# Linear attention and a Swish layer on one core: two groups of VectorE sums exchanged in the Y phase of block 6

## The chip, the cores and the metric

The kernel runs on one core of a Trainium2 chip. A core has five engines that run side by side, each with its own in-order queue: TensorE (PE, with its weight loads as PEld), VectorE (DVE), ScalarE (ACT), GpSimd (POOL) and SyncE (SP, which here only issues transfers). The metric is the device time in microseconds, the median of several runs of a kernel. The types that go in and out are float32; inside, the kernel works in bfloat16 with float32 sums.

## What is computed

Two layers, one behind the other. The first is a linear attention over 8 batches, 8 heads, 576 positions and a head size of 64; its result, laid out as 4608 tokens by 512, goes through a layer with 2048 hidden features.

```python
def phi(x): return np.where(x > 0, x, np.exp(x) - 1.0) + 1.0
q_p, k_p = phi(q), phi(k)
kv  = np.einsum('bhsd,bhse->bhde', k_p, v)
z   = np.sum(k_p, axis=2)
num = np.einsum('bhsd,bhde->bhse', q_p, kv)
den = np.einsum('bhsd,bhd->bhs', q_p, z)[..., None] + 1e-06
x   = (num / den) as 4608 x 512
h   = x @ w_in                          # 512 x 2048
g   = h * (1.0 / (1.0 + np.exp(-beta * h)))
out = g @ w_out                         # 2048 x 512
```

## The kernel before

**Blocks.** A batch has 576 = 9 x 64 positions. Eight ninths of a batch, 512 tokens, make one block, so blocks 0 to 7 are the batches 0 to 7; the last ninths of all eight batches together make block 8. The loop that starts at line 1074 runs b from 1 to 8 (B is 8). Each pass has two phases: H (`h_fast`, or `h_phase` for b = 1 and 2), which makes g from x, and Y (`y_fast`), which makes the output from g. The attention of a later batch is woven in: while block b runs, batch b + 1 gets its x (`numer_all`), and batch b + 2 its phi.

**How work is placed.** The order on each engine's queue is the order in which the program writes the instructions (`manual_schedule`); waits across engines follow from the data. Side work is put into two dictionaries, `sh` for the H phase and `sy` for the Y phase: `at(sy, n, f)` files f under slot n, and `run(side, n)` emits what lies there at a fixed point of the phase. So "slot 0 of Y" is a place in the program, and for VectorE's instructions a place in VectorE's queue.

**Products of sums.** Both matrix products save multiplications by a Strassen-like scheme: the operands are cut into halves, sums and differences of the halves are made on VectorE, and seven half-size products stand in for eight. In Y, all features take part. In H, from block 3 on, a part of the features does: the quarter 0 of w_in's columns in every block, and in the blocks 7 and 8 the quarter 2 as well (`h_products(b, 0)`, `h_products(b, 2)`). For these the kernel needs two sets of sums:

- `h_w_sums(fq)`, lines 797 to 803: four VectorE instructions that make the sums of w_in's quarter fq. They are made once: quarter 0 in block 2, quarter 2 ("w_in's second part") in the Y phase of block 6. The sums of quarter 2 are laid into the room of `vf`, the float32 buffer of v, which GpSimd's `v_copy` (L244) has read for the last time in block 5. They are first read in the second half of block 7's H phase, as `<-vf`.
- `h_x_sums(b)`, lines 811 to 822: four VectorE instructions (all at L822) that make the sums of block b's x, in the Y phase of the block before. They read `xT` (for block 8 `xT_tail`) and write the room of `xs_sb`. Block 7's H phase starts with a product of these sums: there `p0` (L837, tile `hz`) is the first thing on TensorE, while in the blocks 3 to 6 two full products (L405, tile `h_ps`) go ahead of it.

**Where x comes from.** `numer_all(b + 1)` runs at slot 10 of block b's H phase. VectorE divides (L351) and writes `xs_sb`; then SyncE issues four DMA transposes (L358) that carry `xs_sb` to `xT`. The x sums need their landing, both because they read `xT` and because they overwrite `xs_sb`. GpSimd's `tail_copy` (L371) takes the last ninth out of the same `xT`.

**The Y phase** (`y_fast`). TensorE runs seven products of 16 matmuls each (L1003), in the order ya, yd, ya, yc, yb, yd, yb. ScalarE copies ya into `r1` (L1018). VectorE then makes `u2` = yc + `r1` (L1026) and `u3` = yd + `u2` (L1027). The second use of yd writes the PSUM bank that u3 has read, so TensorE's sixth product waits for L1027. Then follow y2's two sums, L1036 ("the first sum of y") and L1039, and y1's L1047, with the stores between them. Slot 0 lies behind the copy into r1, so on VectorE ahead of u2; slot 4 lies between L1036 and the sixth product, so on VectorE ahead of L1039. Four PSUM banks (ya, yd, yc, yb) are handed on in turn to the first products of the next H phase.

Of the kernel before, what the change touches and what calls it, by code (L numbers as in the profile page):

```python
# [16 lines left out]
def kernel(  # L17
# [12 lines left out]
    B, H, S, D = q.shape  # L30
# [125 lines left out]
    def table(func):  # L156
        nc.scalar.activation(act0, warm[:, 0:1], func)  # L157
# [4 lines left out]
    def phi_exp(b, a, pr, x):  # L162
        e = work.tile([P, 2, J, D], BF16, tag="e", name="e", bufs=4)
        nc.scalar.activation(e, x, ACTF.Exp)  # L164
        st[b, a, pr, "e"] = e

    def phi_relu(b, a, pr, x):
        if pr == 0:
            st[b, a, "r"] = work.tile([P, 2, 2, J, D], BF16, tag="r", name="r")
        r = st[b, a, pr, "r"] = st[b, a, "r"][:, pr]  # L170
        nc.vector.tensor_scalar(r, x, 0.0, 1.0, ALU.max, ALU.add)  # L171

    def phi_tile(b, a):
        st[b, a] = work.tile([P, 2, J, P], BF16, tag=f"phi{a}", name=f"phi_{a}", bufs=1)

    def phi_min(b, a, pr):
        nc.vector.tensor_tensor(  # L177
            st[b, a][:, pr].rearrange("p j (h d) -> p j h d", h=2),
            st[b, a, pr, "e"].rearrange("p h j d -> p j h d"),
            st[b, a, pr, "r"].rearrange("p h j d -> p j h d"),  # L180
            ALU.min,
        )

    def xin(b, a, pr):
        if b == 0:
            return x0f[pr if a == "q" else 2 + pr]
        return (xk if a == "k" else xq)[b % 2][:, 2 * pr : 2 * pr + 2]

    def phi_part(b, a, pr):
        x = xin(b, a, pr)  # L190
        phi_exp(b, a, pr, x)
        phi_relu(b, a, pr, x)
        phi_min(b, a, pr)
# [11 lines left out]
    def v_copy(eng, b, pr):  # L205

        copy(
            eng, vaug[b % 2][:, pr, :, :, 0:D],
            (v0b if b == 1 else vf)[:, 2 * pr : 2 * pr + 2].rearrange("p h j d -> p j h d"),
        )  # L210
# [5 lines left out]
    def kv_both(b):  # L216

        t = banks("kvp")
        for pr in range(2):
            for j in range(J):
                for il in range(2):
                    for a in range(2):
                        nc.tensor.matmul(  # L226
                            t[half(il), a, pr * EA : (pr + 1) * EA],
                            st[b, "k"][half(a), pr, j, il * D : (il + 1) * D],
                            vaug[b % 2][half(a), pr, j, il, 0:EA],
                            start=(j == 0), stop=(j == J - 1), skip_group_check=True,  # L230
                        )
        tv = t[:, :, 0 : 2 * EA].rearrange("p a (r e) -> p a r e", r=2)
        if b > 1:
            nc.vector.tensor_copy(kv_q[b % 2], tv)
            return
        st[b, "kv"] = kv_bd.rearrange("p a r h e -> p a r (h e)")
        for il in range(2):
            copy((nc.scalar, nc.vector)[il], kv_bd[half(il), :, :, il], tv[half(il)])
# [34 lines left out]
    def q_trans_dma(b):  # L273
        st[b, "qTd"] = work.tile([P, 2, 2 * J, G], BF16, tag="qT", name="qTd", bufs=1)
        for hh in range(2):
            nc.sync.dma_start_transpose(
                out=st[b, "qTd"][:, hh],
                in_=st[b, "q"][half(hh)].rearrange("p a j c -> p (a j c)"),
            )
# [90 lines left out]
    def tail_copy(b):  # L370
        nc.gpsimd.tensor_copy(  # L371
            xT_tail[:, :, b].rearrange("p i r n -> p i (r n)"), xT[b % 2][:, :, 8]
        )
# [99 lines left out]
    def w_sum(k):  # L473

        for n in range(2):
            r = slice(4 * n, 4 * n + 4)
            a, b = (
                (wq(n, HM), wq(n, 0)),
                (wq(2 + n, HM), ws[0][:, r]),
                (wq(2 + n, HM), wq(n, HM)),  # L480
                (wq(2 + n, 0), ws[1][:, r]),
            )[k]
            nc.vector.tensor_sub(ws[k][:, r], a, b)
# [253 lines left out]
    def at(side, n, *fs):  # L737
        side.setdefault(n, []).extend(fs)
# [54 lines left out]
    def h_w_plain(fq, f, r):  # L793

        return w_in_sb[fq][:, 2 * r : 2 * r + 2, f * 256 : (f + 1) * 256]

    def h_w_sums(fq):

        s, a = h_w[fq], lambda f, r: h_w_plain(fq, f, r)
        nc.vector.tensor_add(s[:, 0], a(1, 0), a(1, 1))  # L800
        nc.vector.tensor_sub(s[:, 1], s[:, 0], a(0, 0))
        nc.vector.tensor_sub(s[:, 2], a(0, 0), a(1, 0))
        nc.vector.tensor_sub(s[:, 3], a(0, 1), s[:, 1])

    def h_x_plain(b, r, t):

        if b == B:
            return xT_tail[:, :, 4 * t : 4 * t + 4, r]
        return xT[b % 2][:, :, 4 * t + r : 4 * t + 4 : 2]

    def h_x_sums(b):

        t = [h_xs[:, k] for k in range(4)]
        x = lambda r, t: h_x_plain(b, r, t)

        def like(a, c):
            return a.rearrange("p i (t n) -> p i t n", n=c.shape[-1])

        for k, (u, w) in enumerate((
            (x(0, 1), x(0, 0)), (x(1, 1), t[0]), (x(1, 1), x(0, 1)), (x(1, 0), t[1])  # L820
        )):
            nc.vector.tensor_sub(like(t[k], u), u, like(w, u) if k % 2 else w)  # L822
# [236 lines left out]
    def next_loads(b):  # L1059

        for pr in range(2) if b == 2 else ():
            v_copy(nc.gpsimd, b, pr)
        if b + 1 < B:
            if b == 3:
                load_v(b + 1)
            nc.gpsimd.tensor_copy(gate, st[b, "qTd"][:, 1, 2 * J - 1, G - 1 : G])
            if b != 3:
                load_v(b + 1)
            if b > 2:
                load_qk(b + 1)  # L1070
            for pr in range(2) if b > 2 else ():
                v_copy(nc.gpsimd, b + 1, pr)

    for b in range(1, B + 1):
        n, m = b + 1, b + 2
        sh, sy = {}, {}
        if b == 2 or b == B - 1:
            at(sh, 0, lambda: tail_copy(b))
        if n < B:
            at(sh, 0, lambda: next_loads(n))  # L1080
            if b > 2:
                at(sh, 0, lambda: tail_copy(b))
            at(sh, {1: 9, 2: 3}.get(b, 0), lambda: kv_both(n))
            at(sh, {1: 11, 2: 5}.get(b, 10), lambda: numer_all(n))
        if b == 1:
            at(sh, 4, lambda: w_sum(2))
            at(sh, 9, lambda: w_sum(1))
            at(sy, 0, lambda: w_sum(3))
        if m < B:
            at(sy, 0, lambda: phi_tile(m, "q"), lambda: phi_tile(m, "k"))  # L1090
            if b == 1:

                for pr in range(2):
                    at(sy, 0, lambda pr=pr: phi_exp(m, "q", pr, xin(m, "q", pr)))
                    at(sy, 2, lambda pr=pr: phi_relu(m, "q", pr, xin(m, "q", pr)))
                    at(sy, 3 + pr, lambda pr=pr: phi_min(m, "q", pr))
                for pr in range(2):
                    at(sy, 0, lambda pr=pr: v_copy(nc.scalar, m, pr))
                at(sy, 4, lambda: q_trans_dma(m))
                for pr in range(2):  # L1100
                    at(sy, 5, lambda pr=pr: phi_exp(m, "k", pr, xin(m, "k", pr)))
                    at(sy, 5, lambda pr=pr: phi_relu(m, "k", pr, xin(m, "k", pr)))
                    at(sy, 6, lambda pr=pr: phi_min(m, "k", pr))
                at(sy, 6, lambda: table(ACTF.Silu))
            else:
                at(sy, 0, lambda: phi_part(m, "q", 0))
                at(sy, 1, lambda: phi_part(m, "q", 1))
                at(sy, 1, lambda: q_trans_dma(m))
                at(sy, 4, lambda: phi_part(m, "k", 0))
                at(sy, 4, lambda: phi_part(m, "k", 1), lambda: table(ACTF.Silu))  # L1110
        if b == 2:
            at(sh, 2, lambda: h_w_sums(0))
        if b == B - 2:
            at(sy, 4, lambda: h_w_sums(2))
        if 2 <= b < B:
            at(sy, 6 if b < B - 2 else 0, lambda: h_x_sums(n))
        (h_phase if b < 3 else h_fast)(b, xT[b % 2] if b < B else xT_tail, sh)
        y_fast(b, sy)

# [29 lines left out]
```

## Time and profile before

| | us |
|---|---|
| three runs, median | 273.45 |
| lowest, highest | 273.04, 274.24 |
| the profiled execution, its time | 273.47 |
| its span in the profile | 271.7 |

In the profile each time is in microseconds from the start of the span. A row of a timeline reads: start, busy time, engine, line, instruction, result <- operands, shapes, count, and in brackets the idle time of that engine ahead of it with what ended it. A row such as `DVE xs_sb L822` in the chain of waits names the engine, the tile written and the line. The queues of issuing engines carry a q (SPq). The granted clock of TensorE was 0.999 of full speed over the span. Matmuls are pipelined and the profile models their ends, so distances between starts are safer than busy times.

### The profile page before, as it was taken

Reading aid. Unit: us, or ns where it says so; the run is one execution under the profiler, and the core shown is the slowest. Engines: PE = TensorE matmul, PEld = TensorE weight load, DVE = VectorE, ACT = ScalarE, POOL = GpSimd, SP = SyncE. Lnnn points to the kernel's source line nnn. Section 1 sums busy time; section 2 is a strip of 40 time slices with the busy share of each in tenths; the row PEclk is TensorE's granted clock in tenths of the full one; section 3 lists DMA queues with packets and bytes.
Section 4 is the critical chain, followed back from the end, with each engine's and each line's share of the span. In section 5 each row is a group of like instructions: output and inputs, shape, how many; then the busy total and the mean of one; then the engine's idle time right before and its main releaser. Section 6 shows DMA issues by size and latency. Waiting matters only on the chain.

```text
span 271.7 us, 6793 instructions
## 1 busy us (share of the span) xinstructions
PE 263.0 (97%) x2859; PEld 181.3 (67%) x2865; DVE 207.1 (76%) x404; ACT 167.4 (62%) x236; POOL 43.6 (16%) x65
## 2 busy tenths in 40 slices
PE   7799999999999999999999999999999799999994
PEld 3485455446865587658765876588658666886793
DVE  4871786999996579689968986899686877856862
ACT  5738894977965893599349934994492038405810
POOL 5922005040105003030213003310000100000000
PEclk9999999999999999999999999999999999999999
DMA  7999999997599945995699559945504050023013
GB/s 252 240 207 351 249 320 249 273 183 258 90 247 191 187 78 99 281 210 72 109 257 232 85 91 273 232 86 96 148 7 85 0 154 4 0 51 106 0 41 116
DMA packets 49214, 42.19 MB, mean 155 GB/s; under 512 B 30352, under 2 KB 41248, under 8 KB 49184
## 3 DMA queue, kind: packets, MB, share of 16 engines
q0 software_dynamic: 13296, 22.81, 37.3%
q1 hardware_dynamic: 35568, 18.75, 31.0%
q8 instruction: 22, 0.36, 0.5%
q10 hardware_dynamic: 320, 0.20, 0.2%
q14 instruction: 8, 0.07, 0.1%
HBM read 36.71 MB, written 9.44 MB: 170 GB/s over the span
## 4 chain that ended last, share of the span: by engine, by line
PE 89%; DMA 4%; DVE 2%; SPq 2%; issue 1%; ACT 0%; DVEq 0%; ACTq 0%
PE h_ps L405 36%; PE yd L1003 10%; PE ya L1003 9%; PE yb L1003 8%; PE hc L837 5%; PE yc L1003 5%; PE y_ps L420 4%; PE hz L837 4%; DMA stage<-in_k_dram 3%; PE kvp L226 2%; PE nps L336 2%; DMA xT<-xs_sb 2%; PE yb L975 1%; SPq L358 1%; PE xtp L385 1%
## 5 line engine op out<-in xcount | busy, mean ns | idle before, releaser
L413 ACT ACTIVATE g<-h_ps,beta_c 128x512 bf16<-128x512 f32 x112 | 74.6, 690 | 63.0 <-PE h_ps L405 62.5
L405 PE MATMUL h_ps<-xT,w_in 128*128 128x512 bf16 (+1 forms) x464 | 97.6, 357 | 0.1
L405 PEld LDWEIGHTS <-w_in 128*128 128x128 bf16 x496 | 44.8, 98 | 40.7 <-issue 0.2
L1003 PEld LDWEIGHTS <-stage 128*128 128x128 bf16 x480 | 47.0, 98 | 5.5
L1003 PEld LDWEIGHTS <-g 128*128 128x128 bf16 x384 | 37.5, 98 | 7.6 <-issue 1.6
L1003 PE MATMUL ya<-w_out,g 128*128 128x256 bf16 x256 | 30.6, 273 | 0.0
L351 DVE TENSOR_TENSOR xs_sb<-nps,rden 128x448 bf16<-128x448 f32 (+2 forms) x24 | 18.2, 758 | 0.8
L164 ACT ACTIVATE e<-xk 128x1152 bf16<-128x1152 bf16 (+1 forms) x15 | 16.7, 1159 | 0.2 <-DMA xk<-in_k_dram 0.2
L1003 PE MATMUL yd<-ws,g 128*128 128x256 bf16 x128 | 15.3, 273 | 1.4 <-DVE u L1027 1.4
L164 ACT ACTIVATE e<-xq 128x1152 bf16<-128x1152 bf16 x14 | 15.6, 1160 | 0.0
L157 ACT ACT_TABLE_LOAD x12 | 15.4, 1283 | 0.2
L1003 PE MATMUL yc<-ws,stage 128*128 128x256 bf16 x128 | 15.3, 273 | 0.0
L1003 PE MATMUL yd<-ws,stage 128*128 128x256 bf16 x128 | 15.3, 273 | 0.0
L244 POOL CAST vaug<-vf 128x1152 bf16<-128x1152 f32 x10 | 11.4, 1175 | 22.1 <-DMA vf<-in_v_dram 22.1
L420 PE MATMUL y_ps<-w_out,g 128*128 128x512 bf16 x60 | 14.4, 379 | 0.3 <-issue 0.2
L887 ACT ACTIVATE g<-hc,beta_c 128x512 bf16<-128x512 f32 x16 | 10.1, 683 | 6.4 <-DVE hc L873 6.4
L177 DVE TENSOR_TENSOR phi_q<-e,r 128x1152 bf16<-128x1152 bf16 x16 | 12.1, 757 | 2.3 <-ACT e L164 1.3
L177 DVE TENSOR_TENSOR phi_k<-e,r 128x1152 bf16<-128x1152 bf16 x16 | 12.7, 802 | 1.5 <-DVE r L171 0.5
L746 DVE TENSOR_TENSOR stage<-g 128x1024 bf16<-128x1024 bf16 x16 | 11.0, 686 | 3.2 <-ACT g L413 3.2
L1003 PE MATMUL yb<-w_out,stage 128*128 128x256 bf16 x112 | 13.4, 272 | 0.0
L1003 PE MATMUL yb<-ws,stage 128*128 128x256 bf16 x112 | 13.4, 273 | 0.0
L837 PEld LDWEIGHTS <-w_in 128*128 128x128 bf16 x96 | 9.4, 98 | 4.5
(139 smaller groups left out, 359.2 us busy)
## 6 DMA issues: line engine op xcount, KB each, us to landing
out_dram<-y SPq DMA_DIRECT2D x29, 256.0 KB, 3.8
vf<-in_v_dram POOLq DMA_DIRECT2D x6, 1152.0 KB, 9.1
xq<-in_q_dram POOLq DMA_DIRECT2D x7, 576.0 KB, 12.4
xk<-in_k_dram POOLq DMA_DIRECT2D x7, 576.0 KB, 14.5
w_in<-in_moe_w_in_dram POOLq DMA_DIRECT2D x4, 512.0 KB, 11.7
g<-in_moe_w_out_dram POOLq DMA_DIRECT2D x2, 1024.0 KB, 17.2
stage<-in_moe_w_out_dram POOLq DMA_DIRECT2D x2, 1024.0 KB, 20.9
stage<-in_q_dram SPq DMA_DIRECT2D x2, 576.0 KB, 4.2
```

Of the source, the lines that this page charges most:

```text
L157: nc.scalar.activation(act0, warm[:, 0:1], func)
L164: nc.scalar.activation(e, x, ACTF.Exp)
L177: nc.vector.tensor_tensor(st[b, a][:, pr].rearrange("p j (h d) -> p j h d", h=2), st[b, a, pr, "e"].rearrange("p h j d -> p j h d"), st[b, ...
L244: eng.tensor_copy(dst, src)
L351: nc.vector.tensor_mul(xs_sb[:, ils, v0 * D : v1 * D].rearrange("p i (u d) -> p i u d", d=D), pv[:, :, :, 0:D], rden[:, :, :, None].to_bro ...
L405: nc.tensor.matmul(hp[:, c0:c1].rearrange("p (t n) -> p t n", n=n), w_in_sb[ff // 4][:, kc, (ff % 4) * P : (ff % 4 + 1) * P], xm, start=(k ...
L413: nc.scalar.activation(g_sb[b % 2][:, ff, :], hp, ACTF.Silu, scale=beta_c[:, ff : ff + 1])
L420: nc.tensor.matmul(yp[:, c0:c1], g_sb[b % 2][:, ff, t * P : (t + 1) * P], w_out_sb[i][:, c, c0:c1], start=(ff == 0), stop=(ff == FC - 1), ...
L746: nc.vector.tensor_add(gs[0][:, c], g[:, c, HM:512], g[:, c2, HM:512])
L837: nc.tensor.matmul(o, lhs[:, i, a * P : (a + 1) * P], m, start=(first and a == 0 and i == 0), stop=True, skip_group_check=True,)
L887: nc.scalar.activation(g_sb[b % 2][:, ff].rearrange("p (t n) -> p t n", t=2), src, ACTF.Silu, scale=beta_c[:, ff : ff + 1],)
L1003: nc.tensor.matmul(ps[:, p * HM : (p + 1) * HM], lhs(c, p), rhs(c), start=(first and p == 0 and c == 0), stop=True, skip_group_check=True,)
```

## The change

In the Y phase of block 6 the two groups of VectorE sums change places. The sums of w_in's quarter 2 go from slot 4 to slot 0, and the sums of block 7's x from slot 0 to slot 4. In the Y phase of block 7 the sums of block 8's x stay in slot 0, and in the blocks 2 to 5 the x sums stay in slot 6.

```diff
         if b == B - 2:
-            at(sy, 4, lambda: h_w_sums(2))
+            at(sy, 0, lambda: h_w_sums(2))
         if 2 <= b < B:
-            at(sy, 6 if b < B - 2 else 0, lambda: h_x_sums(n))
+            at(sy, {B - 2: 4, B - 1: 0}.get(b, 6), lambda: h_x_sums(n))
```

## The prediction

> **What bounds the kernel now.** I read the page's engine shares and its chain of work first, then the chain piece by piece around the Y phase of block 6, then the timelines of VectorE, SyncE and TensorE there, and last block 7, which already has the order that block 6 is to get. From the page, engine shares and the chain:
>
> ```profile
> span 271.7 us, 6793 instructions
> PE 263.0 (97%) x2859; PEld 181.3 (67%) x2865; DVE 207.1 (76%) x404; ACT 167.4 (62%) x236; POOL 43.6 (16%) x65
> ...
> PE 89%; DMA 4%; DVE 2%; SPq 2%; issue 1%; ACT 0%; DVEq 0%; ACTq 0%
> ```
>
> TensorE bounds the kernel; only some 11% of the chain lies elsewhere. The columns of the chain in order of time are start, length (both us), and what:
>
> ```profile
> 206.28 4.34 DMA xT<-xs_sb
> ...
> 210.74 0.44 DVE xs_sb L822
> ...
> 212.37 0.61 DVE u L1026
> ...
> 213.01 0.70 DVE u L1027
> ...
> 213.75 1.91 PE yd L1003 x16
> 215.66 1.75 PE yb L1003 x16
> 217.41 0.44 PE hz L837 x4
> ```
>
> Here the chain leaves TensorE: the transposes of batch 7's x land at about 210.62, VectorE's four x sums (L822) follow, then u2 (L1026) and u3 (L1027), and only then TensorE's yd product starts. The timelines of the three engines, with the waits in brackets (VectorE, SyncE, TensorE; start, busy us):
>
> ```profile
> 207.38 0.69 DVE L748 TENSOR_TENSOR stage<-g,stage 128x1024 bf16<-128x1024 bf16 x1
> ...
> 210.74 0.43 DVE L822 TENSOR_TENSOR xs_sb<-xT 128x512 bf16<-128x512 bf16 x1 [2.67 <-DMA xT<-xs_sb]
> 211.20 0.50 DVE L822 TENSOR_TENSOR xs_sb<-xT,xs_sb 128x512 bf16<-128x512 bf16 x1
> ...
> 212.29 0.68 DVE L1026 TENSOR_TENSOR u<-yc,r 128x512 f32<-128x512 f32 x1
> 213.01 0.69 DVE L1027 TENSOR_TENSOR u<-yd,u 128x512 f32<-128x512 f32 x1
> 213.79 0.69 DVE L1036 TENSOR_TENSOR y<-yb,u 128x512 f32<-128x512 f32 x1
> 214.40 0.41 DVE L800 TENSOR_TENSOR vf<-w_in 128x512 bf16<-128x512 bf16 x1
> ...
> 215.52 0.42 DVE L803 TENSOR_TENSOR vf<-w_in,vf 128x512 bf16<-128x512 bf16 x1
> 215.86 0.69 DVE L1039 TENSOR_TENSOR y<-yd,u 128x512 f32<-128x512 f32 x1
> ```
>
> ```profile
> 202.39 5.15 SPq L358 DMA_TRANSPOSE xT<-xs_sb  x4
> ```
>
> ```profile
> 208.69 1.91 PE L1003 MATMUL yc<-ws,stage 128*128 128x256 bf16 x16
> 210.44 1.91 PE L1003 MATMUL yb<-ws,stage 128*128 128x256 bf16 x16
> 213.75 1.91 PE L1003 MATMUL yd<-ws,g 128*128 128x256 bf16 x16 [1.40 <-DVE u L1027]
> 215.50 1.91 PE L1003 MATMUL yb<-w_out,stage 128*128 128x256 bf16 x16
> 217.24 0.60 PE L837 MATMUL hz<-xs_sb,h_w 128*128 128x256 bf16 x4
> ```
>
> VectorE ends its g sums at 207.38 + 0.69 = 208.07 and stands 2.67 us with x sums at its head that wait for the landing. TensorE pays for 1.40 us of that. The profile models the ends of matmuls, so I count by starts: yc to yb is 210.44 - 208.69 = 1.75 us for 16 matmuls, but yb to yd is 213.75 - 210.44 = 3.31 us. The stall is worth 3.31 - 1.75 = **1.56 us**. Block 7, same timelines, where the x sums at this place are of data long landed:
>
> ```profile
> 234.69 0.69 DVE L748 TENSOR_TENSOR stage<-g,stage 128x1024 bf16<-128x1024 bf16 x1
> 235.30 0.42 DVE L822 TENSOR_TENSOR xs_sb<-xT_tail 128x512 bf16<-128x512 bf16 x1
> ...
> 236.43 0.42 DVE L822 TENSOR_TENSOR xs_sb<-xT_tail,xs_sb 128x512 bf16<-128x512 bf16 x1
> 237.25 1.91 PE L1003 MATMUL yb<-ws,stage 128*128 128x256 bf16 x16
> 237.52 0.69 DVE L1026 TENSOR_TENSOR u<-yc,r 128x512 f32<-128x512 f32 x1 [0.67 <-PE yc L1003]
> 238.25 0.69 DVE L1027 TENSOR_TENSOR u<-yd,u 128x512 f32<-128x512 f32 x1
> 239.00 1.91 PE L1003 MATMUL yd<-ws,g 128*128 128x256 bf16 x16
> 239.20 0.69 DVE L1036 TENSOR_TENSOR y<-yb,u 128x512 f32<-128x512 f32 x1 [0.26 <-PE yb L1003]
> ```
>
> There u2 starts 0.27 us behind the start of yb, u3 0.73 behind u2, and yd starts 239.00 - 237.25 = 1.75 us behind yb: no stall.
>
> **The change part by part.** Nothing is added: VectorE's four x sums and four w sums of block 6 change places; no matmul, DMA or wait of another engine's own is new.
>
> *The w sums, to the place ahead of u2.* They need only w_in, loaded at the start, and the room in vf, last read by POOL's copies of batch 7's v, long ago:
>
> ```profile
> 172.51 2.24 POOL L244 CAST vaug<-vf 128x1152 bf16<-128x1152 f32 x2 [7.10 <-DMA vf<-in_v_dram]
> ...
> 210.74 0.69 POOL L371 COPY xT_tail<-xT 128x256 bf16<-128x256 bf16 x1 [27.39 <-DMA xT<-xs_sb]
> ```
>
> So they should start at 208.07 + 0.04. They last from 214.40 to 215.52 + 0.42 = 215.94 today, 1.54 us, and would end at 209.65. Queued behind them is u2, which can't start before 210.44 + 0.27 = 210.71, when yc is done. They lie wholly in a 2.6 us gap, with 1.06 us to spare: cost nothing. Without that cover each 0.1 us past 1.06 would be 0.1 us on yd.
>
> *u2 and u3.* u2 at 210.71, u3 at 211.44, ended 212.13; in block 6 today yd follows the end of u3 (213.01 + 0.69 = 213.70) by 0.05, so u3 allows yd at 212.18, and TensorE's own pace allows it at 210.44 + 1.75 = 212.19. This is the tightest place of the forecast, 0.01 us, but block 7's rows carry the same distances without a stall. yd moves from 213.75 to 212.19: gain 1.56.
>
> *The x sums, behind y2's first sum.* L1036 starts 0.20 us behind yd in block 7, so 212.39; but u3 has VectorE until 212.13, so it isn't held up, and the next instruction starts 214.40 - 213.79 = 0.61 later, at 213.00. The landing (210.62) is 2.4 us past by then, so the wait has gone, not moved. The sums take 236.43 + 0.42 - 235.30 = 1.55 us in block 7 and end at 214.55. Who waits? First, block 7's opening product hz (L837), which reads the second sum: it is due 217.24 - 213.75 = 3.49 us behind yd, at 215.68, 1.1 us after the last sum. Second, y's sum L1039, queued behind them on VectorE: yd's result is ready at 212.19 + 1.75 + 0.20 = 214.14, so it starts about 0.4 us late, at 214.55, and ends at 215.24. That sets back an output store, on which nothing waits, and a PSUM bank that block 7's first full h_ps reuses; this one starts behind the four hz matmuls (0.44 us by the chain), at 216.12, 0.88 us later. Today the w sums stand at this same spot with nearly the same length, so this is no new burden. Cost nothing; gone cover would cost what exceeds 0.88 us.
>
> *A neighbour that is new.* POOL's tail copy starts when the transposes land, at 210.74, beside the x sums today and beside u2 (210.71) afterwards. Today's x sums beside it took 0.43 and 0.50 us, 0.42 in block 7. Block 1 shows u2 beside such a copy (timeline):
>
> ```profile
> 73.21 0.69 DVE L1026 TENSOR_TENSOR u<-yc,r 128x512 f32<-128x512 f32 x1 [0.26 <-PE yc L1003]
> 73.26 0.40 POOL L371 COPY xT_tail<-xT 128x256 bf16<-128x256 bf16 x1 [11.46 <-DMA xT<-xs_sb]
> ```
>
> u2 keeps its 0.69 us. The price lies between nothing and the copy's whole 0.69 us; I take nothing, by block 1's row, the same pair of instructions. The Trainium skill's page "SBUF — State Buffer" (section "Who interferes with whom") speaks of this pair of engines: a VectorE instruction with two inputs in SBUF and a GpSimd one that reads SBUF exclude each other for a whole instruction, while one with at most one SBUF input outside the 2-port modes doesn't contend. u2 reads one operand from PSUM, so by that rule too the sum stays at 1.56; the same rule would have today's x sum or the copy wait out the other, whereas the rows show both starting at 210.74, with at most some tenths of a microsecond added to either.
>
> *Behind it.* From 213.75 on, by stages (busy time of PE, PEld, DVE, ACT, POOL, the granted clock, DMA share and rate):
>
> ```profile
> 213.75:268.00 54.25, 54.19 (x448) 42.46 (x447) 38.79 (x65) 22.42 (x36) 0.00 (x0) 1.00 0.16 46
> ```
>
> TensorE is busy 54.19 of 54.25 us at full clock, so what starts 1.56 us earlier ends 1.56 us earlier; the transfers left in that stretch are stores.
>
> **The sum.** Profiled execution: 273.47 us (span 271.7, 1.77 around it). 273.47 - 1.56 + 0 + 0 + 0 = 271.91. The median of the runs shown is 273.45, 0.02 below the profiled one, so I predict **271.9 us**.
>
> **The rivals.**
>
> *Part of the gain is lost at u2 (chance 0.07).* POOL's copy holds u2 for up to 0.69 us; u3 has no slack, so yd comes that much later: gain 0.87, 272.6 us. For it: the 0.01 us of margin, and the lengthened copy (0.69 against 0.40). Against it: the rows of block 1.
>
> *The stall was hidden anyway (0.05).* If something later had been waiting with a time of its own, the 1.56 us would turn into a new gap in block 7, and the time would stay at 273.4. For it: the tail ends in stores, and VectorE is 76% busy. Against it: the stage row above, where TensorE never rests, and L1039 as the last thing that the swap sets back, with 0.88 us of room.
>
> *The w sums block VectorE's queue (0.06): slower.* VectorE is in order. Its first w sum carries a wait today that costs nothing, because all is over by 213.8 (the instructions of that line):
>
> ```profile
> L800 DVEq EVENT_SEMAPHORE  x1: 21/21/21, 213.8 to 213.8; - x1
> ```
>
> At 208.07 it could be unmet. The one late event of the neighbourhood is POOL's tail copy, which ends at 210.74 + 0.69 = 211.43. If the wait covered it, the sums would run 211.47 to 213.01, u2 and u3 (213.70 - 212.29 = 1.41 us) to 214.42 and yd start at 214.47, 0.72 later than now: 274.2 us. It decides from 209.16 on (u2's 210.71 less 1.55 us): a wait that lasts beyond costs one for one, and makes the kernel slower than now once it passes 210.74. Against it: the vf room was last read at 172.51 + 2.24 = 174.75, and the tail copy of batch 7 stands later in the program than these sums.
>
> *The change doesn't do what it says:* only if slot 0 were emitted elsewhere; it is run behind ya's copy and ahead of pd, as L822 shows by its present place. No chance of its own.
>
> **How the numbers follow.** The forecast has 0.82, the rivals 0.07, 0.05 and 0.06. A measurement of this kernel can tell about 0.5%, or 1.37 us, from no change, and 1.56 lies just above it. The three runs before span 1.2 us (273.04 to 274.24), and the landing that ended the stall took 4.34 us in this one execution; where it takes less, the old kernel stalls less. I give the forecast 0.78 to be seen above the bound: 0.82 x 0.78 = 0.64 faster. The rest of it, 0.18, with 0.07 and 0.05, is 0.30 within the bound, and 0.06 slower. The range: the three runs less 1.56 give 271.5 to 272.7, the first rival 272.6; I widen the ends by 0.2 for the unknown state of the landing: 271.3 to 272.9. Outside lie most of the 0.05 and 0.06 and about a tenth of the forecast.
>
> **What would show it.** In the changed profile: four sums vf<-w_in starting near 208.1 with no wait worth naming, u2 near 210.7 ended by yc, no gap ahead of yd (1.75 us behind yb), x sums near 213.0 without a wait for the DMA, hz 5.24 us behind yb's start, and a span near 270.1. A wait of VectorE ahead of the w sums, a u2 over 0.7 us or started late, or a gap ahead of hz or h_ps of block 7 would show the rivals, and a chain that leaves TensorE again later than yd would prove the forecast wrong.

## The result, and the profile after

| | before | after |
|---|---|---|
| runs, median (lowest to highest), us | 273.31 (273.04 to 274.24), 6 runs | 271.78 (271.67 to 271.92), 6 runs |
| ratio after / before, 95% interval | | 0.9944 (0.9934 to 0.9954) |
| profiled execution, time and span, us | 273.47 and 271.7 | 271.76 and 270.0 |

The kernel became 1.53 us faster by the medians, 0.56%; the forecast was 271.9 us. Below, one run is left out of its median: with both groups in slot 4, one of six runs took 276.74 us, at a granted clock of 0.994. The page of the changed kernel:

```profile
span 270.0 us, 6793 instructions
PE 263.6 (98%) x2859; PEld 181.8 (67%) x2865; DVE 206.5 (77%) x404; ACT 167.4 (62%) x236; POOL 43.0 (16%) x65
```

The instruction counts are those of before. The busy times differ by 0.6 us at most; TensorE's share of the shorter span has grown from 97% to 98%, VectorE's from 76% to 77%. The chain of waits of the changed kernel around block 6's Y phase (start, length, what):

```profile
208.70 1.75 PE yc L1003 x16
210.45 1.75 PE yb L1003 x16
212.20 1.75 PE yd L1003 x16
213.94 1.75 PE yb L1003 x16
215.69 0.44 PE hz L837 x4
```

Where SyncE, the landing and VectorE stood in the chain before, it now runs through TensorE without a break. Its timeline, VectorE, POOL and TensorE together (start, busy us, waits in brackets):

```profile
207.22 0.69 DVE L748 TENSOR_TENSOR stage<-g,stage 128x1024 bf16<-128x1024 bf16 x1
207.83 0.42 DVE L800 TENSOR_TENSOR vf<-w_in 128x512 bf16<-128x512 bf16 x1
...
208.96 0.42 DVE L803 TENSOR_TENSOR vf<-w_in,vf 128x512 bf16<-128x512 bf16 x1
210.29 1.91 PE L1003 MATMUL yb<-ws,stage 128*128 128x256 bf16 x16
210.56 0.69 DVE L1026 TENSOR_TENSOR u<-yc,r 128x512 f32<-128x512 f32 x1 [1.18 <-PE yc L1003]
210.59 0.40 POOL L371 COPY xT_tail<-xT 128x256 bf16<-128x256 bf16 x1 [27.44 <-DMA xT<-xs_sb]
211.28 0.69 DVE L1027 TENSOR_TENSOR u<-yd,u 128x512 f32<-128x512 f32 x1
...
212.03 1.91 PE L1003 MATMUL yd<-ws,g 128*128 128x256 bf16 x16
212.24 0.69 DVE L1036 TENSOR_TENSOR y<-yb,u 128x512 f32<-128x512 f32 x1 [0.26 <-PE yb L1003]
212.84 0.41 DVE L822 TENSOR_TENSOR xs_sb<-xT 128x512 bf16<-128x512 bf16 x1
...
213.97 0.42 DVE L822 TENSOR_TENSOR xs_sb<-xT,xs_sb 128x512 bf16<-128x512 bf16 x1
214.30 0.68 DVE L1039 TENSOR_TENSOR y<-yd,u 128x512 f32<-128x512 f32 x1
...
215.53 0.60 PE L837 MATMUL hz<-xs_sb,h_w 128*128 128x256 bf16 x4
```

The w sums start straight behind the last g sum. u2 now waits for TensorE (1.18 us), not TensorE for u2: yd stands 212.03 - 210.29 = 1.74 us behind yb, where it was 3.31. The landing still comes at about the same place, as POOL's copy at 210.59 shows, but VectorE reaches the x sums 2.3 us after it.

The span fell by 1.7 us, somewhat more than the stall. The rest is not of the change: the Y phase of block 6 itself began earlier (ya at 203.30 against 203.45). The two rows, before and after:

```profile
203.45 1.91 PE L1003 MATMUL ya<-w_out,g 128*128 128x256 bf16 x16
```

```profile
203.30 1.91 PE L1003 MATMUL ya<-w_out,g 128*128 128x256 bf16 x16
```

The stretch from that ya to the end of the span leaves this out: 271.7 - 203.45 = 68.25 us before, 270.0 - 203.30 = 66.70 after, so **1.55 us** for the change. Below, "Y6 to the end" is this stretch. Spans are given to 0.1 us, so a stretch is good to about 0.05 us and a difference of two to about 0.1.

### The profile page after: what moved, and what is told of

Read it like the earlier page. It is cut to its first block, busy times and chain, and to the rows that moved or that the text cites. A ratio compares the mean times of both kernels' runs of the same rounds, so it can differ in the third digit from the quotient of the medians.

```text
span 270.0 us, 6793 instructions
## 1 busy us (share of the span) xinstructions
PE 263.6 (98%) x2859; PEld 181.8 (67%) x2865; DVE 206.5 (77%) x404; ACT 167.4 (62%) x236; POOL 43.0 (16%) x65
## 4 chain that ended last, share of the span: by engine, by line
PE 94%; DVE 2%; DMA 1%; ACT 1%; issue 1%; DVEq 0%
PE h_ps L405 36%; PE ya L1003 10%; PE yd L1003 10%; PE yb L1003 9%; PE hc L837 5%; PE yc L1003 5%; PE y_ps L420 5%; PE hz L837 4%; PE kvp L226 2%; PE nps L336 2%; DMA stage<-in_q_dram 1%; PE yb L975 1%; PE xtp L385 1%; DVE r L171 1%; DVE phi_q L177 1%
## 5 line engine op out<-in xcount | busy, mean ns | idle before, releaser
L413 ACT ACTIVATE g<-h_ps,beta_c 128x512 bf16<-128x512 f32 x112 | 74.5, 689 | 61.6 <-PE h_ps L405 61.2
L177 DVE TENSOR_TENSOR phi_q<-e,r 128x1152 bf16<-128x1152 bf16 x16 | 12.1, 757 | 2.3 <-ACT e L164 1.3
L177 DVE TENSOR_TENSOR phi_k<-e,r 128x1152 bf16<-128x1152 bf16 x16 | 12.7, 802 | 1.5 <-DVE r L171 0.5
```

Source lines behind the costliest of these rows:

```text
L177: nc.vector.tensor_tensor(st[b, a][:, pr].rearrange("p j (h d) -> p j h d", h=2), st[b, a, pr, "e"].rearrange("p h j d -> p j h d"), st[b, ...
L413: nc.scalar.activation(g_sb[b % 2][:, ff, :], hp, ACTF.Silu, scale=beta_c[:, ff : ff + 1])
```

## The experiments

The diffs are against the kernel before, except where it says against the change. The runs were made in three groups, on three chips, each beside its own runs of the kernel before: the w sums alone, the old order without the landing, both groups in slot 4 and slot 6 (before: median 273.98); slot 5, the w sums twice and the two repeats of before (273.57); the last two of the table (273.71). The times in the expectations start from the 273.3 and 271.8 us above, and all three groups ran slower than that; so it is the ratios and the stretch that answer them.

| kernel | yb to yd | Y6 to the end | median | ratio to before (95%) |
|---|---|---|---|---|
| before | 3.31 | 68.25 | 273.31 | |
| the change | 1.74 | 66.70 | 271.78 | 0.9944 (0.9934 to 0.9954) |
| w sums early, x sums stay | 3.20 | 68.08 | 273.85 | 0.9996 (0.9984 to 1.0007) |
| old order, no landing needed | 1.75 | 66.73 | 272.54 | 0.9951 (0.9937 to 0.9965) |
| both groups in slot 4 | 1.74 | 66.75 | 272.33 | 0.9944 (0.9928 to 0.9960) |
| x sums in slot 6 | 1.75 | 68.41 | 274.06 | 1.0004 (0.9992 to 1.0015) |
| x sums in slot 5 | 1.75 | 66.69 | 272.26 | 0.9950 (0.9937 to 0.9963) |
| w sums twice in slot 0 | 1.94 | 66.89 | 272.71 | 0.9963 (0.9951 to 0.9975) |
| x sums, then w sums three times, in slot 4 | 1.75 | 69.59 | 275.52 | 1.0073 (1.0048 to 1.0099) |
| both groups in slot 0, x first | 4.97 | 69.92 | 276.69 | 1.0102 (1.0066 to 1.0138) |

### Which part of the change pays

**The w sums alone to slot 0.**

```diff
-            at(sy, 4, lambda: h_w_sums(2))
+            at(sy, 0, lambda: h_w_sums(2))
```

> The w sums alone go to slot 0, ahead of the x sums, which stay there. Theory (the whole gain is the x sums' wait for the landing, taken off VectorE's way to u2; the w sums only fill a gap): the x sums still wait until about 210.6, u2 and u3 follow them, yd stands as far behind yb as before (about 3.3 us), and the time is that of the kernel before, 273.3 us (within 0.3). Rival (it is the w sums' leaving the place behind u3 that pays, since it frees VectorE for the sums of y): most of the gain is there, about 271.8 us.

The time is that of before. Its timeline:

```profile
211.21 1.91 PE L1003 MATMUL yb<-ws,stage 128*128 128x256 bf16 x16
211.40 0.69 POOL L371 COPY xT_tail<-xT 128x256 bf16<-128x256 bf16 x1 [27.30 <-DMA xT<-xs_sb]
211.40 0.43 DVE L822 TENSOR_TENSOR xs_sb<-xT 128x512 bf16<-128x512 bf16 x1 [1.09 <-DMA xT<-xs_sb]
...
214.41 1.91 PE L1003 MATMUL yd<-ws,g 128*128 128x256 bf16 x16 [1.29 <-DVE u L1027]
```

The w sums fill 1.5 us of VectorE's idle time (its wait shrinks from 2.67 to 1.09), and TensorE gains nothing by it: work put into a wait that another thing ends is free, and worthless.

**The x sums alone to slot 4, behind the w sums.**

```diff
-            at(sy, 6 if b < B - 2 else 0, lambda: h_x_sums(n))
+            at(sy, {B - 2: 4, B - 1: 0}.get(b, 6), lambda: h_x_sums(n))
```

> Only the x sums move; the w sums stay in slot 4, ahead of them, so that eight sums stand between L1036 and L1039. Theory: yd follows yb by 1.75 us, so the stall of before is gone, but L1039 ends near 216.45 where the first h_ps of block 7 is due at 215.96 on the bank that L1039 reads, which gives back 0.5 to 0.8 us: 272.3 to 272.6 us, with a new gap of TensorE ahead of that h_ps. Rival (VectorE has room enough there, and moving the x sums alone is the whole of it): 271.8 us.

The expectation failed, and the rival held: nothing was given back, 66.75 us. Moving the x sums alone is worth as much as the whole change. The timeline shows why the expected stall is missing:

```profile
216.32 0.69 DVE L1039 TENSOR_TENSOR y<-yd,u 128x512 f32<-128x512 f32 x1
216.51 1.03 PE L405 MATMUL h_ps<-xT,w_in 128*128 128x512 bf16 x4
...
218.31 0.69 DVE L854 TENSOR_TENSOR h_u<-hc,h_u 128x512 f32<-128x512 f32 x1
219.11 0.60 PE L837 MATMUL hc<-xs_sb,h_w 128*128 128x256 bf16 x4
```

The first h_ps of block 7 starts at 216.51 while L1039 still runs until 217.01. So it doesn't use the PSUM bank that L1039 reads, as the forecast had supposed, and the four banks are not handed on in the order ya, yd, yc, yb in which the section on the kernel lists them.

**The old order without the landing.** Sums of data that has long landed, into a free buffer:

```diff
+    h_alt = xk[0].rearrange("p i j d -> p (i j d)")[:, 0:2048].rearrange("p (k i n) -> p k i n", k=4, i=2)
...
-        t = [h_xs[:, k] for k in range(4)]
-        x = lambda r, t: h_x_plain(b, r, t)
+        t = [(h_alt if b == B - 1 else h_xs)[:, k] for k in range(4)]
+        x = lambda r, t: h_x_plain(B - 2 if b == B - 1 else b, r, t)
...
-        s, t = ([a[:, k] for k in range(4)] for a in (h_w[fq], h_xs))
+        s, t = ([a[:, k] for k in range(4)] for a in (h_w[fq], h_alt if b == B - 1 else h_xs))
```

> The order of the kernel before, but batch 7's x sums are made of batch 6's x and written to a free buffer, so that they need no landing; block 7's products thus take sums of the wrong batch. Theory: with the wait gone the order itself costs nothing; the x sums run from about 208.1 to 209.7, yd starts 1.75 us behind yb, and the time is 271.8 us (within 0.3). Rival (the four sums ahead of u2, or their meeting POOL's tail copy, cost time by themselves in the old order): 272.5 us or more, up to the 273.3 of before.

```profile
208.80 0.42 DVE L822 TENSOR_TENSOR xk<-xT 128x512 bf16<-128x512 bf16 x1
...
211.25 1.91 PE L1003 MATMUL yb<-ws,stage 128*128 128x256 bf16 x16
...
211.52 0.69 DVE L1026 TENSOR_TENSOR u<-yc,r 128x512 f32<-128x512 f32 x1 [1.17 <-PE yc L1003]
...
213.00 1.91 PE L1003 MATMUL yd<-ws,g 128*128 128x256 bf16 x16
```

yd follows yb by 1.75 us and Y6 to the end is 66.73: the whole gain, with the order of before. The median of 272.54 lies 0.4 above the 272.1 that was expected at most; against the runs of before that it was measured beside, 273.98, the ratio agrees with that of the change. Not the place of the x sums cost the time, but their wait for the landing ahead of u2. The rival's second half, their meeting POOL's tail copy, is not in this run, where the copy starts at 211.74, beside u2. Its price stands in the rows: from the first to the fourth x sum's start it is 1.22 us beside the copy (before) and 1.13 here, so 0.09 us at most of the 1.56.

**Work behind the landing.** Both groups in slot 0, the x sums first:

```diff
-            at(sy, 4, lambda: h_w_sums(2))
+            at(sy, 0, lambda: h_x_sums(n), lambda: h_w_sums(2))
-        if 2 <= b < B:
+        if 2 <= b < B and b != B - 2:
```

> Both groups in slot 0, the x sums first, so that the w sums stand behind the wait for the landing and ahead of u2. Theory (VectorE work behind the landing and ahead of u2 costs one for one): yd moves 1.46 us further back than before, to 4.75 us behind yb; the span counted from the start of block 6's Y phase is 69.7 us instead of 68.25, the time about 1.5 us over that of the kernel before. Rival (the stall is bounded by something else than VectorE's queue): as before, 68.25 us.

```profile
211.67 1.91 PE L1003 MATMUL yb<-ws,stage 128*128 128x256 bf16 x16
212.17 0.69 POOL L371 COPY xT_tail<-xT 128x256 bf16<-128x256 bf16 x1 [28.46 <-DMA xT<-xs_sb]
212.17 0.42 DVE L822 TENSOR_TENSOR xs_sb<-xT 128x512 bf16<-128x512 bf16 x1 [2.87 <-DMA xT<-xs_sb]
...
216.64 1.91 PE L1003 MATMUL yd<-ws,g 128*128 128x256 bf16 x16 [3.06 <-DVE u L1027]
```

Each microsecond of VectorE behind the landing and ahead of u2 costs one: yd stands 4.97 us behind yb, 1.66 more than before, of which 1.46 are the w sums and 0.20 a later landing (the x sums start 0.50 us behind yb's start, 0.30 before). With the run of the w sums alone this makes a pair: the same four sums cost nothing ahead of the wait and their whole length behind it. The medians differ by more than the 1.5 us expected, 2.98 us. The four runs spread from 275.29 to 277.09, and the profiled one came to Y6 1.2 us later than the first trace of before (204.68 against 203.45), which the stretch leaves out; whether that is the whole of the difference is not shown.

### How much room the new places have

**The w sums twice** (against the change):

```diff
             at(sy, 0, lambda: h_w_sums(2))
+            at(sy, 0, lambda: h_w_sums(2))
```

> As the change, but the four w sums of slot 0 are made twice. Theory (u2 has about 1.2 us to spare in the changed kernel, so the first 1.2 us of VectorE's work ahead of it are free and what exceeds costs one for one): the second four end near 210.85 where u2 was due at 210.56, so u2 and yd are 0.2 to 0.3 us late: 272.0 us. Rival (each sum ahead of u2 costs its length): 1.5 us more, 273.3 us. Rival (u2 has room beyond that, since yd isn't held by u3): 271.8 us.

```profile
211.10 1.91 PE L1003 MATMUL yb<-ws,stage 128*128 128x256 bf16 x16
211.24 0.42 DVE L803 TENSOR_TENSOR vf<-w_in,vf 128x512 bf16<-128x512 bf16 x1
211.39 0.52 POOL L371 COPY xT_tail<-xT 128x256 bf16<-128x256 bf16 x1 [28.11 <-DMA xT<-xs_sb]
211.57 0.68 DVE L1026 TENSOR_TENSOR u<-yc,r 128x512 f32<-128x512 f32 x1
```

u2 starts 0.47 us behind yb's start instead of 0.27, and yd 1.94 instead of 1.74: 0.20 us late for 1.47 us of added work. In the changed kernel the last w sum starts at 208.96, an instruction behind it can start 0.33 us later (as u2 does here, 211.57 - 211.24), and u2 starts at 210.56: so 1.27 us were free, and the 0.20 us beyond cost one for one.

**The x sums in slot 5 and in slot 6** (against the change; 5 or 6 for the 4):

```diff
-            at(sy, {B - 2: 4, B - 1: 0}.get(b, 6), lambda: h_x_sums(n))
+            at(sy, {B - 2: 5, B - 1: 0}.get(b, 6), lambda: h_x_sums(n))
```

> As the change, but the x sums go to slot 5, behind both sums of y2. Theory: L1039 runs at about 214.0, the x sums follow at 214.6, the second ends near 215.5, as hz is due at 215.53: 0 to 0.15 us lost, 271.8 to 271.95 us. Rival (hz waits for all four sums, which end near 216.1): 0.6 us lost, 272.4 us.

> As the change, but the x sums go to slot 6, behind the last sum of y. Theory (the forecast's claim that block 7's opening product hz is the next to wait for the x sums): L1047 can't start before 215.73, the second x sum ends near 217.2, hz starts there instead of at 215.53, and the 1.7 us come back: 273.5 us (within 0.3), with the stall of TensorE ahead of hz. Rival (hz reads them late enough, or other work fills in): 271.8 to 272.3 us.

Slot 5 costs nothing (66.69), but it is the last such place: there the second x sum ends at 215.97 and hz starts at 216.04. Its ratio, 0.9950, carries the same start-up scatter as the others. Slot 6 gives everything back (68.41):

```profile
216.77 0.42 DVE L822 TENSOR_TENSOR xs_sb<-xT,xs_sb 128x512 bf16<-128x512 bf16 x1
217.11 0.42 DVE L822 TENSOR_TENSOR xs_sb<-xT 128x512 bf16<-128x512 bf16 x1
...
217.25 0.61 PE L837 MATMUL hz<-xs_sb,h_w 128*128 128x256 bf16 x4 [1.58 <-DVE xs_sb L822]
217.45 0.42 DVE L822 TENSOR_TENSOR xs_sb<-xT,xs_sb 128x512 bf16<-128x512 bf16 x1
```

hz starts behind the second sum, with the fourth still to come. The x sums have a window: behind u3, and with the second of them ended before hz is due.

**The sums of y late.** As the bank was not where the forecast had put it, this run looked for what is late next:

```diff
-            at(sy, 4, lambda: h_w_sums(2))
+            at(sy, 4, lambda: h_x_sums(n), *[lambda: h_w_sums(2)] * 3)
-        if 2 <= b < B:
-            at(sy, 6 if b < B - 2 else 0, lambda: h_x_sums(n))
+        if 2 <= b < B and b != B - 2:
+            at(sy, {B - 1: 0}.get(b, 6), lambda: h_x_sums(n))
```

> Slot 0 is empty; slot 4 holds the x sums and then the four w sums three times over, so that L1039 runs about 4.4 us later than in the changed kernel and ends about 7.3 us behind the start of the sixth product, yd. Where is the PSUM bank that L1039 has read used next? Theory 1 (after the run with both groups in slot 4, where L1039 ended 0.5 us behind the start of the first h_ps and nothing waited): the second h_ps of block 7, due 5.67 us behind yd, waits, 1.7 us or somewhat more are lost, and the span counted from the start of block 6's Y phase goes from 66.7 to about 68.4 us or more. Theory 2 (as the forecast had it): the first h_ps, due 3.93 us behind yd, waits, and 3.4 us are lost: 70.1 us. Rival: neither waits, 66.7 us.

```profile
213.25 1.91 PE L1003 MATMUL yd<-ws,g 128*128 128x256 bf16 x16
...
217.18 1.03 PE L405 MATMUL h_ps<-xT,w_in 128*128 128x512 bf16 x4
...
218.98 1.02 PE L405 MATMUL h_ps<-xT,w_in 128*128 128x512 bf16 x4
...
219.90 0.69 DVE L1039 TENSOR_TENSOR y<-yd,u 128x512 f32<-128x512 f32 x1
...
221.89 0.69 DVE L854 TENSOR_TENSOR h_u<-hc,h_u 128x512 f32<-128x512 f32 x1
222.63 0.60 PE L837 MATMUL hc<-xs_sb,h_w 128*128 128x256 bf16 x4 [2.63 <-DVE h_u L854]
```

All three expectations missed the place. Neither the first nor the second h_ps waits for L1039: both have started before it (217.18 and 218.98 against 219.90). What waits is hc's second product in block 7's H phase, and not for a bank of y: it waits for L854, block 7's own sum, which stands behind all of this in VectorE's queue. The loss is 69.59 - 66.70 = 2.89 us for L1039 being later by (219.90 - 213.25) - (214.30 - 212.03) = 4.38 us, so some 1.5 us of delay are free. The run with both groups in slot 4 agrees from the other side: it delays L1039 by 1.47 us, L854 ends at 219.00, hc starts at 219.11, which is just its due time (6.53 us behind yd, as in the changed kernel). That place is full; the changed kernel has the 1.5 us in hand.

Where the changed kernel uses L1039's bank next, this run does not decide, because the banks were handed out differently in it. In the traces of before, of the change and of both groups in slot 4, the first matmul of the second h_ps waits for VectorE's semaphore (`$S[101]`, which L1039 raises). Here it waits for ScalarE's (`$S[103]`, raised by L413, which reads the first h_ps), and it starts 5.73 us behind yd instead of 5.67. So in the changed kernel the second h_ps may still follow L1039, which ends 2.7 us ahead of it there (214.98 and 217.70); the trace names the semaphore, not the instruction. The 1.5 us do not hang on this: with both groups in slot 4, where the second h_ps waits for VectorE as in the changed kernel, neither it nor hc is late for the 1.47 us of delay.

### The spread of the runs

> The kernel before once more, for its trace: where do the x sums start, against the start of yb, and how long is the stall ahead of yd? Theory (the stall is set by the landing): yb to yd is 1.75 us plus what the x sums' start exceeds the point 1.28 us ahead of yb's start, and the span differs from that of the first trace by the difference of the landings. Rival: the span varies for other reasons and the stall is 1.56 us again.

> The same a second time: the landing and the stall move together, or the spread of the times of before (273.04 to 274.24) has another source.

Two more traces of before, with 273.50 and 273.88 us and spans of 271.7 and 272.1. One row of each:

```profile
210.76 0.42 DVE L822 TENSOR_TENSOR xs_sb<-xT 128x512 bf16<-128x512 bf16 x1 [2.67 <-DMA xT<-xs_sb]
```

```profile
211.14 0.42 DVE L822 TENSOR_TENSOR xs_sb<-xT 128x512 bf16<-128x512 bf16 x1 [2.66 <-DMA xT<-xs_sb]
```

VectorE's wait is 2.67, 2.67 and 2.66 us in the three traces, and yb to yd 3.31, 3.30 and 3.31: the stall hardly varies from run to run, and the rival held. Y6 to the end is 68.25, 68.22 and 68.24. What varies is when Y6 begins (203.45, 203.48, 203.86), and the difference is there already in block 1: its copy into r1 (L1018) starts at 68.27 us in the first trace of before, at 68.63 in the third and at 69.49 in the run with both groups in slot 0. Which of the start-up's loads or waits makes it was not tried.

## Why the prediction was right, step by step

- *The stall and its size.* Right. 1.56 us were forecast from the distances between starts; 1.55 were found in the stretch that holds the change (good to about 0.1), 1.53 in the medians. The idle time that the profile gives ahead of yd (1.40) would have been too small, since the matmul ahead of it is modelled past its start-to-start distance.
- *Its cause.* Right, and shown from three sides: the wait taken away in the old order gives the gain (66.73), the x sums moved alone give it (66.75), the w sums moved alone don't (68.08).
- *The w sums ahead of u2 cost nothing.* Right. They started without a wait, so the rival in which they block VectorE's queue did not come about; u2 had 1.18 us to spare where 1.06 were worked out, and doubling them cost only the excess.
- *u2 to yd, the tightest place.* Right: 1.74 us, no stall, though the margin was 0.01 us on paper.
- *POOL's copy beside u2.* Right, at no cost: u2 took 0.69 us and the copy 0.40. Beside the x sums the copy takes 0.69 and the second x sum 0.50 (the run with the w sums alone early, too). This is the pairing that the Trainium skill's page "SBUF — State Buffer", section "Who interferes with whom", gives: an instruction with one operand in PSUM left the copy alone, one with two in SBUF didn't. The forecast read the equal starts (210.74) as speaking against the Trainium skill's exclusion; that reading fails, since the wait lies inside the record, as a later end and not as a later start. The Y phase of block 5 shows it, where batch 6's tail copy meets L177, a VectorE instruction of 0.76 us with both operands in SBUF. First both groups in slot 4, where neither is ahead, then the w sums twice, where the copy is ahead:

```profile
182.70 0.76 DVE L177 TENSOR_TENSOR phi_q<-e,r 128x1152 bf16<-128x1152 bf16 x1
182.70 1.02 POOL L371 COPY xT_tail<-xT 128x256 bf16<-128x256 bf16 x1 [7.38 <-DMA xT<-xs_sb]
```

```profile
182.88 0.40 POOL L371 COPY xT_tail<-xT 128x256 bf16<-128x256 bf16 x1 [6.87 <-DMA xT<-xs_sb]
182.98 0.91 DVE L177 TENSOR_TENSOR phi_q<-e,r 128x1152 bf16<-128x1152 bf16 x1
```

In the traces of the change, of the w sums alone early and of before, L177 starts 0.07, 0.14 and 0.29 us ahead of the copy, which takes 0.95, 0.88 and 0.73 us: in all four it ends 1.02 us behind the start of L177, however late it started. Beside the sums of block 6, too, it ends 0.69 us behind an x sum that starts with it and 0.67 behind a w sum that starts 0.15 us ahead (the w sums twice). So one holds the other up for most of its length, whichever comes first.
- *The x sums behind L1036, and hz as the next to wait.* Right: at yd + 0.81 as worked out, hz unhindered at yd + 3.50; slot 6 shows the price of missing it.
- *The cover behind L1039.* Wrong in its reason and size, without effect on the time. The step "a PSUM bank that block 7's first full h_ps reuses", with 0.88 us of room, fell: that h_ps ran while L1039 was still at work. The room is about 1.5 us, and it is L854, further back in VectorE's queue, that TensorE waited for where L1039 was made late. That this cost the forecast nothing owes nothing to the 0.88: L1039 starts 2.27 us behind yd, against 2.11 before, and the 0.16 us between lie far inside either room.
- *The chance that the gain stays within 0.5%.* I had put part of the spread down to the landing. The three traces show the landing steady and the spread at the start of the kernel, so the gain itself was safer than the forecast made it. The bound lay close all the same: the interval of the measured gain, 0.46% to 0.66%, reaches below 0.5%.

## What to carry to other kernels

An in-order queue turns one unmet wait into a wait of everything behind it: look for the instruction at the head of an idle engine's queue, and ask who needs it soonest and who needs what stands behind it. Here TensorE needed the x sums 3.5 us later than the u3 that they held up (hz at yd + 3.50). Where kernels differ by 0.5% and start-up scatters as much, compare the stretch that holds the change, from start to start, with the rest left out; and check a supposed reuse of a buffer by making its reader late, before counting on its margin. Look then whether the next user still waits for the same engine, since a changed program may be given its buffers in another order.

## What was not expected of the hardware

The last transposes of batch 7's x landed at nearly the same distance from yb's start in every trace: the x sums that waited for them began 0.30, 0.29 and 0.30 us behind it in the three traces of before, and 0.19 and 0.50 in two other orders of the same work. In the other seven traces POOL's copy, which waits for the same landing, began 0.23 to 0.49 us behind it. The start of the kernel was far looser: in the twelve traces block 1's copy into r1 starts between 67.97 and 69.49 us.

Nor was it expected that VectorE and POOL hold each other up inside their records, while both start at the same time; the rows stand above, under POOL's copy beside u2.
